# Fifteen one-word reads at the end of the first pass and seven one-word stores behind the last store of a channel-attention kernel

## The chip, the cores and the metric

The kernel runs on one core of a Trainium2 chip. The metric is the device time of one execution in microseconds (us). Runs of one kernel are told by their median, and one further execution is recorded by the hardware profiler, instruction by instruction. Times inside the profile count from the start of its span.

## What is computed

An image x of 384 x 384 pixels with 384 channels (bfloat16, 113 MB) is scaled channel by channel. The scale comes from the mean and the maximum of each channel over all pixels, through a small two-layer net:

```python
def reference(x, w1, w2):
    B, H, W, C = x.shape
    xf = x.reshape(B, H * W, C)
    gap = jnp.mean(xf, 1)
    gmp = jnp.amax(xf, 1)
    h_a = gap @ w1
    h_a = h_a * (lambda x, dt: x.astype(dt))(h_a > 0, h_a.dtype)
    h_m = gmp @ w1
    h_m = h_m * (lambda x, dt: x.astype(dt))(h_m > 0, h_m.dtype)
    scale = _sigmoid(h_a @ w2 + h_m @ w2)
    return x * scale[:, None, None, :]
```

No output can be written before the last pixel has been read. So x has to be read once for the scale, and whatever of it could not be kept in on-chip memory has to be read again.

## The kernel before

The 147,456 pixels lie as 1152 rows in each of 128 partitions (a "row" below is 384 channels, 768 bytes, in each partition). On-chip memory holds about 290 rows at a time, so the kernel makes two passes.

**First pass (loop at L363 to L396).** A list called steps is written out ahead of time: loads of blocks of rows into places of one large buffer (rows), and between them tests and packings. For each load the SP queue issues one transfer (L371). PE adds the rows up into a PSUM bank (L274) and DVE takes the running maximum into acc (L340), both as the load lands. One part of x (224 rows) is packed on the fly to seven blocks of 24 rows in place of 32 and stays on chip; its check and packing are ACT's and PE's work (L301, L302, L322, L328, L329). The order of every engine's instructions is that of the program text. There are 53 loads. Towards the end they get smaller, down to 2 to 11 rows, and they stay on chip for the second pass. The last four of them (SUM_TAIL) are summed by other matmuls (L290), and ahead of the last two (FOLD_BEFORE) DVE begins to fold acc (L355 to L357).

**The joint (L399 to L431).** The weights are loaded, acc is folded to one row, turned over by PE, reduced by DVE, and the small net gives z; ACT's sigmoid writes scale_bc (L431). Rows whose places were needed meanwhile (acc's own, and one block more) are read again (L412, L415).

**Second pass (L440 to L581).** DVE multiplies each block by scale_bc (L436), ACT's queue stores it (L445, L451, L490), and SP's queue reads the rows that were not kept (L529), each into a place whose store has landed. Packed blocks are unpacked between them by DVE (L468, L473) and ACT (L487). Three large stores of unpacked blocks go out among the last three blocks, and two small stores (L580, L581) come last. Behind these stands a branch (L582) that is entered only if the packing was not exact for some value; it reads a flag that the first pass computed.

**Queues and semaphores.** Loads are issued by SP, stores by ACT, each in program order. Every transfer, on either queue, signals its landing on one of eight semaphores (DMAHW0 to DMAHW7), which transfers take in turn in the order of the program. A transfer is issued when the one that had its semaphore before, eight places earlier, has landed, and when its other waits (a place to come free, say) are over:

```python
        _, block, rows, lo, hi = st
        m = hi - lo
        nc.sync.dma_start(out=rows, in_=rows_of(xr, block)[:, lo:hi, :])
...
    for to, block in leaving:
        store(to, block, 0)
    with tc.If(bad != 0):
```

Of the kernel before, what the change touches and what calls it, by code (L numbers as in the profile page):

```python
# [12 lines left out]
BF16 = mybir.dt.bfloat16  # L13
# [67 lines left out]
OTHER_PLACES = ((1, 17, (14,)), (2, 10, (24,)))  # L81
TEST_SCALE = 0.031187
SUM_TAIL = 4
MM_ROWS = 4


@with_exitstack
def kernel(
# [7 lines left out]
    nc = tc.nc  # L96
    P = nc.NUM_PARTITIONS
# [9 lines left out]
    xr = x.rearrange("b h w c -> (b h w) c")  # L107
    orr = out.rearrange("b h w c -> (b h w) c")

    def rows_of(ap, block):  # L110
        first, n = block
        return ap[first * P:(first + n) * P, :].rearrange("(p n) c -> p n c", n=n)

    consts = ctx.enter_context(tc.tile_pool(name="consts", bufs=1, side="right"))
# [5 lines left out]
    def take(n):  # L120
        nonlocal at
        at += n
        return at - n, n

    for_psum = PSUM_ROWS + BANK_ROWS
    first_block = take(for_psum + A)
# [14 lines left out]
    small = consts.tile([P, 16], BF16)  # L141
# [41 lines left out]
    late = words_ps[:, 0:LATE_ROWS, :]  # L183
    sum_ps = bank_a[0:NQP, 0:MM_ROWS * P]
    tp_ps = [
# [72 lines left out]
    loads = [st for st in steps if st[0] == "load"]  # L258
    tail_rows = sum(st[4] - st[3] for st in loads[len(loads) - SUM_TAIL:])

# [9 lines left out]
    def sums(rows, n, done, total):  # L270
        for k in range(0, n, MM_ROWS):
            g = min(MM_ROWS, n - k)
            for q in range(CQ):
                nc.tensor.matmul(  # L274
                    sum_ps[q * QP:q * QP + 1, 0:g * P],
                    lhsT=ones_bf[:, 0:1],
                    rhs=rows[:, k:k + g, q * P:(q + 1) * P],
                    start=(done + k == 0),
                    stop=(done + k + g == total),
                )  # L280

    def turn_sums():
        for r in range(MM_ROWS):
            nc.scalar.copy(out=s_sb[r % 2], in_=sum_ps[:, r * P:(r + 1) * P])  # L284
            nc.tensor.matmul(gsum_ps, lhsT=s_sb[r % 2], rhs=pick, start=(r == 0), stop=False)

    def tail_sums(rows, n, last):
        for k in range(n):
            for q in range(CQ):
                nc.tensor.matmul(  # L290
                    gsum_ps[:, q:q + 1], lhsT=rows[:, k, q * P:(q + 1) * P], rhs=ones_bf,
                    start=False, stop=(last and k == n - 1 and q == CQ - 1),
                )
# [12 lines left out]
    def test(i, what):  # L306

        if what == 2:
            test_one(high(part(i, 3), I8), 5 * i + 4)
            return  # L310
        n = G * C // 2
        a_b = homes[i][:, 0:2 * G, :].rearrange("p (r n) c -> p r (n c)", r=2).bitcast(I8)
        test_one(a_b[:, :, 2 * n * what + 1:2 * n * (what + 1):2], 5 * i + 2 * what)
        test_one(high(part(i, 2), I8)[:, n * what:n * (what + 1)], 5 * i + 2 * what + 1)

    def pack(i, half):
        n = G * C // 2
        span = slice(half * n, (half + 1) * n)
        for c in range(0, n, BANK):
            for r in range(4):  # L320
                for k, dt in enumerate((E4, E3)):
                    nc.tensor.matmul(  # L322
                        words[:, c:c + BANK], lhsT=weights[2 * r + k],
                        rhs=high(part(i, r), dt)[:, half * n + c:half * n + c + BANK],
                        start=(r == 0 and k == 0), stop=(r == 3 and k == 1),
                    )
        for r in (0, 1):
            nc.scalar.copy(out=high(part(i, r), U8)[:, span], in_=low(part(i, r + 2), U8)[:, span])  # L328
        nc.scalar.activation(  # L329
            out=part(i, 2).rearrange("p n c -> p (n c)").bitcast(U16)[:, span], in_=words,  # L330
            func=ACT.Copy, bias=32767.5,
        )

    def judge():
        nc.scalar.activation(out=test_copy, in_=tests[:, 0:NT], func=ACT.Copy, accum_out=test_sum)
        nc.scalar.copy(out=total, in_=test_sum)
        nc.tensor.matmul(bad_ps, lhsT=total, rhs=ones_bf, start=True, stop=True)

    def maximum(out_, in0, in1):
        nc.vector.tensor_tensor(out=out_, in0=in0, in1=in1, op=ALU.max)  # L340

    def turn_over(out_, rows):

        for r in range(LATE_ROWS):
            for q in range(CQ):
                nc.tensor.transpose(  # L346
                    out=out_[:, r, q * P:(q + 1) * P], in_=rows[:, r, q * P:(q + 1) * P], identity=ident_bf
                )
# [3 lines left out]
    def fold():  # L352

        n = folds[-1]
        h = n // 2  # L355
        maximum(acc[:, 0:h, :], acc[:, 0:h, :], acc[:, n - h:n, :])
        folds.append(n - h)  # L357

    done = turn = nth = 0
    for st in steps:  # L360
        if st[0] == "test":
            test(*st[1:])
        elif st[0] == "pack":  # L363
            pack(*st[1:])
        elif st[0] == "judge":
            judge()
        if st[0] != "load":
            continue
        _, block, rows, lo, hi = st
        m = hi - lo  # L370
        nc.sync.dma_start(out=rows, in_=rows_of(xr, block)[:, lo:hi, :])  # L371
        if nth < len(loads) - SUM_TAIL:
            sums(rows, m, done, TOT - tail_rows)
        else:
            tail_sums(rows, m, nth == len(loads) - 1)
        if nth == len(loads) - FOLD_BEFORE:
            fold()
        halves = HALVES if len(folds) == 1 else ((0, folds[-1]),)
        j = max(0, min(m, A - done))
        if j:  # L380
            nc.vector.tensor_copy(out=acc[:, done:done + j, :], in_=rows[:, 0:j, :])
        done += m
        if nth == len(loads) - SUM_TAIL - 1:
            turn_sums()
        while j < m:
            c, e = halves[turn % len(halves)]
            turn += 1
            e = min(e, c + m - j)
            maximum(acc[:, c:e, :], acc[:, c:e, :], rows[:, j:j + e - c, :])
            j += e - c  # L390
        if block == late_block:
            turn_over(late, rows)
        elif block == first_block:
            nc.vector.tensor_copy(out=kept_ps.bitcast(U32), in_=rows[:, 0:PSUM_ROWS, :].bitcast(U32))
            nc.vector.tensor_copy(out=kept_b.bitcast(U32), in_=rows[:, PSUM_ROWS:for_psum, :].bitcast(U32))
        nth += 1  # L396
# [37 lines left out]
    def multiply(dst, src):  # L434
        n = dst.shape[1]
        nc.vector.tensor_tensor(  # L436
            out=dst, in0=src, in1=scale_bc.unsqueeze(1).to_broadcast([P, n, C]), op=ALU.mult
        )
# [50 lines left out]
    def store(buf, block, lo):  # L489
        nc.scalar.dma_start(out=rows_of(orr, block)[:, lo:lo + buf.shape[1], :], in_=buf)  # L490
# [88 lines left out]
    assert not again and not order and not jobs  # L579
    for to, block in leaving:  # L580
        store(to, block, 0)  # L581
    with tc.If(bad != 0):  # L582
        for i in range(PACKED):
            for buf, lo in ((homes[i], FIRST_AT[i]), (homes_d[i], FOURTH_AT[i])):
                n = buf.shape[1]
                nc.sync.dma_start(out=buf, in_=rows_of(xr, packed_block)[:, lo:lo + n, :])
                multiply(buf, buf)
                store(buf, packed_block, lo)
# [30 lines left out]
```

## Time and profile before

| what | value |
|---|---|
| median of 3 runs | 725.78 us (725.48 to 726.16) |
| profiled execution, its own time | 725.41 us |
| span of the profile | 723.6 us |
| busy: DVE, ACT, PE | 564.1, 349.8, 184.7 us |
| read from DRAM, written to DRAM | 192.14 MB, 113.25 MB |
| mean rate over the span | 422 GB/s |
| granted clock of TensorE, mean | 0.616 |
| last load of the first pass issued | 255.65 us |
| scale_bc written | from 275.68 us, 0.49 us |
| last store issued | 681.52 us |

How to read what follows: in the strips the span, or a window of it, is cut into 40 equal slices, and a digit is the busy share in tenths (9 is 90% or more); DMA is the mean over the core's 16 DMA engines. The chain is the work that ended last, followed back from the end. In a list of waits, "A <- B: 36.6, 12, 11.6" says that A's engine stood 36.6 us in all for B, 12 times, at most 11.6 us. SPq and ACTq are the queues of SP and ACT that issue transfers. The trace also holds each update of a semaphore; a load or store makes 16 of them, one by one as its parts land.

### The profile page before, as it was taken

Reading aid. Unit: us, or ns where it says so; the run is one execution under the profiler, and the core shown is the slowest. Engines: PE = TensorE matmul, PEld = TensorE weight load, DVE = VectorE, ACT = ScalarE, POOL = GpSimd, SP = SyncE. Lnnn points to the kernel's source line nnn. Section 1 sums busy time; section 2 is a strip of 40 time slices with the busy share of each in tenths; the row PEclk is TensorE's granted clock in tenths of the full one; section 3 lists DMA queues with packets and bytes.
Section 4 is the critical chain, followed back from the end, with each engine's and each line's share of the span. In section 5 each row is a group of like instructions: output and inputs, shape, how many; then the busy total and the mean of one; then the engine's idle time right before and its main releaser. Section 6 shows DMA issues by size and latency. Waiting matters only on the chain.

```text
span 723.6 us, 3882 instructions
## 1 busy us (share of the span) xinstructions
PE 184.7 (26%) x1363; PEld 74.2 (10%) x1363; DVE 564.1 (78%) x445; ACT 349.8 (48%) x251; POOL 0.7 (0%) x6
## 2 busy tenths in 40 slices
PE   5577475965867470000000000000000000001000
PEld 1222122322322140000000000000000000001000
DVE  5699899999999998797966554897888889495200
ACT  6999999997999200056230023806154442200000
POOL 0000000000000000000000000000000000000000
PEclk9888878896988555555555555555555555555555
DMA  9999999999999979999999999999999999999997
GB/s 380 434 438 435 417 442 427 429 430 432 431 426 428 426 312 356 400 433 431 433 431 431 434 428 431 434 430 435 430 429 432 437 432 430 430 433 439 442 426 339
DMA packets 20403, 305.63 MB, mean 422 GB/s; under 512 B 2624, under 2 KB 2976, under 8 KB 7200
## 3 DMA queue, kind: packets, MB, share of 16 engines
q1 hardware_dynamic: 13040, 192.14, 62.3%
q10 hardware_dynamic: 7344, 113.25, 36.6%
q8 instruction: 10, 0.16, 0.1%
q14 instruction: 9, 0.07, 0.0%
HBM read 192.14 MB, written 113.25 MB: 422 GB/s over the span
## 4 chain that ended last, share of the span: by engine, by line
DMA 63%; DVE 25%; issue 3%; PE 2%; ACT 1%; SPq 0%; DVEq 0%; ACTq 0%
DMA rows<-in_x_dram 40%; DMA out_dram<-rows 23%; DVE acc L340 16%; DVE rows L436 9%; PE words_ps L322 1%; ACT rows L328 0%; DVE acc L436 0%; SPq L371 0%; PE bank_a L274 0%; ACT rows L329 0%; ACT rows L487 0%; PE bank_a L430 0%; ACT scale_bc L431 0%; DVE small L424 0%; PE bank_a L423 0%
## 5 line engine op out<-in xcount | busy, mean ns | idle before, releaser
L436 DVE TENSOR_TENSOR rows<-rows,scale_bc 128x9216 bf16<-128x9216 bf16 (+9 forms) x56 | 230.9, 4164 | 91.2 <-DMA rows<-in_x_dram 90.0
L340 DVE TENSOR_TENSOR acc<-acc,rows 128x2304 bf16<-128x2304 bf16 (+4 forms) x227 | 245.0, 1154 | 13.9 <-DMA rows<-in_x_dram 13.6
L487 ACT COPY rows<-rows 128x1536 uint8<-128x1536 uint8 x28 | 41.3, 1476 | 204.2 <-DVE rows L436 144.8
L274 PE MATMUL bank_a<-rows,small 128*1 128x512 bf16 (+3 forms) x897 | 93.3, 466 | 80.9 <-DMA rows<-in_x_dram 76.1
L346 PE MATMUL words_ps<-ident_bf,acc 128*128 128x128 bf16 x24 | 2.7, 310 | 376.3 <-DVE acc L574 376.3
L301 ACT ACTIVATE rows<-rows 128x3072 uint8<-128x3072 int8 (+1 forms) x35 | 81.9, 2341 | 9.1 <-DMA rows<-in_x_dram 8.4
L302 ACT ACTIVATE rows<-rows 128x3072 uint8<-128x3072 uint8 (+1 forms) x35 | 82.0, 2344 | 1.1
L487 ACT COPY rows<-acc 128x1536 uint8<-128x1536 uint8 x42 | 60.5, 1473 | 18.2 <-DVE acc L473 17.7
L274 PEld LDWEIGHTS <-small 128*1 128x1 bf16 x897 | 30.6, 95 | 140.3 <-issue 118.2
L346 PEld LDWEIGHTS <-acc 128*128 128x128 bf16 x24 | 2.5, 144 | 376.7 <-DVE acc L574 376.7
L322 PE MATMUL words_ps<-rows,scale_bc 128*128 128x512 fp8e4 (+1 forms) x126 | 37.9, 414 | 9.2 <-ACT rows L329 9.2
L328 ACT COPY rows<-rows 128x1536 uint8<-128x1536 uint8 x28 | 39.7, 1468 | 0.4 <-PE words_ps L322 0.4
L322 PE MATMUL words_ps<-rows 128*128 128x512 fp8e3 (+1 forms) x126 | 35.8, 394 | 0.0
L468 DVE TENSOR_SCALAR rows<-rows 128x1536 uint16<-128x1536 uint16 x56 | 31.3, 560 | 1.9
L322 PE MATMUL words_ps<-rows,w_sb 128*128 128x512 fp8e3 x84 | 27.0, 405 | 0.0
L487 ACT COPY acc<-rows 128x1536 uint8<-128x1536 uint8 x14 | 20.5, 1466 | 0.0
L329 ACT ACTIVATE rows<-words_ps 128x1536 uint16<-128x1536 f32 x14 | 20.1, 1439 | 0.0
L322 PEld LDWEIGHTS <-scale_bc 128*128 128x128 bf16 x126 | 12.2, 103 | 30.2 <-issue 19.3
L322 PEld LDWEIGHTS <-rows 128*128 128x128 bf16 x126 | 12.9, 102 | 16.7 <-issue 3.3
L473 DVE SCALAR_TENSOR_TENSOR acc<-acc,rows 128x768 uint32<-128x768 uint32 x14 | 13.4, 959 | 0.5
L473 DVE SCALAR_TENSOR_TENSOR rows<-rows 128x768 uint32<-128x768 uint32 x14 | 13.4, 958 | 0.5
L284 ACT COPY w_sb<-bank_a 65x128 f32<-65x128 f32 x2 | 0.5, 261 | 24.5 <-PE bank_a L274 24.0
(61 smaller groups left out, 72.0 us busy)
## 6 DMA issues: line engine op xcount, KB each, us to landing
rows<-in_x_dram SPq DMA_DIRECT2D x16, 2880.0 KB, 25.4
out_dram<-rows ACTq DMA_DIRECT2D x15, 2880.0 KB, 22.8
rows<-in_x_dram SPq DMA_DIRECT2D x15, 2304.0 KB, 20.0
out_dram<-rows ACTq DMA_DIRECT2D x14, 2304.0 KB, 21.1
rows<-in_x_dram SPq DMA_DIRECT2D x4, 3072.0 KB, 31.8
out_dram<-rows ACTq DMA_DIRECT2D x2, 4608.0 KB, 46.7
rows<-in_x_dram SPq DMA_DIRECT2D x9, 768.0 KB, 16.7
rows<-in_x_dram SPq DMA_DIRECT2D x2, 3264.0 KB, 26.4
```

The lines of the kernel that those rows point to most:

```text
L274: nc.tensor.matmul(sum_ps[q * QP:q * QP + 1, 0:g * P], lhsT=ones_bf[:, 0:1], rhs=rows[:, k:k + g, q * P:(q + 1) * P], start=(done + k == 0 ...
L301: nc.scalar.activation(out=out_, in_=rows, func=ACT.Square, bias=test_bias, scale=TEST_SCALE)
L302: nc.scalar.activation(out=out_, in_=out_, func=ACT.Square, bias=minus4, accum_out=tests[:, k:k + 1],)
L322: nc.tensor.matmul(words[:, c:c + BANK], lhsT=weights[2 * r + k], rhs=high(part(i, r), dt)[:, half * n + c:half * n + c + BANK], start=(r ...
L328: nc.scalar.copy(out=high(part(i, r), U8)[:, span], in_=low(part(i, r + 2), U8)[:, span])
L329: nc.scalar.activation(out=part(i, 2).rearrange("p n c -> p (n c)").bitcast(U16)[:, span], in_=words, func=ACT.Copy, bias=32767.5,)
L340: nc.vector.tensor_tensor(out=out_, in0=in0, in1=in1, op=ALU.max)
L346: nc.tensor.transpose(out=out_[:, r, q * P:(q + 1) * P], in_=rows[:, r, q * P:(q + 1) * P], identity=ident_bf)
L436: nc.vector.tensor_tensor(out=dst, in0=src, in1=scale_bc.unsqueeze(1).to_broadcast([P, n, C]), op=ALU.mult)
L468: nc.vector.tensor_scalar(out=u16(dst), in0=u16(src), scalar1=s1, scalar2=s2, op0=op0, op1=op1)
L473: nc.vector.scalar_tensor_tensor(out=u32(v), in0=u32(v), scalar=0x3F3F3F3F, in1=u32(m), op0=ALU.bitwise_xor, op1=ALU.bitwise_xor)
L487: nc.scalar.copy(out=dst, in_=src)
```

## The change

Two lists are added, a small tile and a small tensor in DRAM. Behind five of the last 20 loads of the first pass (the 20th, 18th, 17th, 14th and 12th from the end), SP issues three reads each. A read takes one word (two bfloat16 channels) of x into each of k partitions, every eighth one from the first on; k goes over 1 to 15. The words land in probe_sb, a column of its own for each read, and nothing uses them. Behind the last store, ACT issues seven stores of one word from each of k = 2, 4, ... 14 partitions of the tile small into the scratch tensor probe_dram. The computation and the output stay the same.

```diff
+PROBES = {20: (1, 2, 3), 18: (5, 6, 7), 17: (9, 10, 11), 14: (13, 14, 15), 12: (4, 8, 12)}
+PROBES_AT_END = (2, 4, 6, 8, 10, 12, 14)
...
+    probe_sb = consts.tile([P, 40], BF16)
+    probe_dram = nc.dram_tensor("probe", [P, 40], BF16).ap()
+    probed = 0
+
+    def probe(k):
+        nonlocal probed
+        c = 2 * probed
+        probed += 1
+        nc.sync.dma_start(
+            out=probe_sb[0:8 * k:8, c:c + 2], in_=rows_of(xr, first_block)[0:8 * k:8, 0, 2 * probed:2 * probed + 2]
+        )
+
     done = turn = nth = 0
...
         nc.sync.dma_start(out=rows, in_=rows_of(xr, block)[:, lo:hi, :])
+        for k in PROBES.get(len(loads) - nth, ()):
+            probe(k)
         if nth < len(loads) - SUM_TAIL:
...
     for to, block in leaving:
         store(to, block, 0)
+    for i, k in enumerate(PROBES_AT_END):
+        c = 2 * i
+        nc.scalar.dma_start(out=probe_dram[0:8 * k:8, c:c + 2], in_=small[0:8 * k:8, 2:4])
     with tc.If(bad != 0):
```

Each of the 22 added transfers takes a semaphore of the eight in its turn.

## The prediction

> **What bounds the kernel now.** I read the strips of the page first, then the split of the chain, then windows of both ends of the change. The profiled execution took 725.41 us (its span 723.6 us, 1.8 us around it); the median of the three runs is 725.78, so this execution stands 0.37 us below it.
>
> ```profile
> DVE  5699899999999998797966554897888889495200
> DMA  9999999999999979999999999999999999999997
> GB/s 380 434 438 435 417 442 427 429 430 432 431 426 428 426 312 356 400 433 431 433 431 431 434 428 431 434 430 435 430 429 432 437 432 430 430 433 439 442 426 339
> ...
> DMA 63%; DVE 25%; issue 3%; PE 2%; ACT 1%; SPq 0%; DVEq 0%; ACTq 0%
> ```
>
> The DMA engines are busy in every slice (18 us each) and move about 430 GB/s, except in the two or three slices from 253 us on: the joint between the passes. So the time is transfers, end to end, plus that joint. The reads of the change lie just before the joint, the stores behind the last transfer. Both places need a look of their own. First the windows (busy us, with counts, of each engine, then PE clock, DMA share, GB/s):
>
> ```profile
> core 0: us, PE busy (x) PEld busy (x) DVE busy (x) ACT busy (x) POOL busy (x), PEclk, DMA share, GB/s
> ...
> 240.00:264.00 24.00, 13.55 (x97) 3.81 (x96) 23.13 (x23) 0.19 (x1) 0.00 (x0) 0.50 1.01 424
> 264.00:277.00 13.00, 8.05 (x111) 7.15 (x105) 10.75 (x17) 1.78 (x7) 0.00 (x0) 0.50 0.65 222
> ```
>
> In the last 24 us of the first pass DMA is full, but DVE has 23.13 busy us too. The chain through the joint tells which is later:
>
> ```profile
> 267.02 1.03 DVE acc L340 x2
> 268.05 0.02 issue
> 268.07 1.17 DVE acc L340
> 269.24 0.02 issue
> 269.26 1.37 DVE acc L340
> 270.63 0.04 DVEq L340
> ```
>
> It is DVE after DVE. Beside it I set each load's last semaphore update. The load issued at 242.80 landed at 258.15, and DVE was free for it at 258.55; the next at 260.46 against 260.89; the last two at 267.16 and 268.33 against 269.2 and 270.6. So a load may land **0.40 us** later here at no cost, the last two over 2 us.
>
> Third, the drain of the load queue, 264 to 280 us in slices of 0.4 us:
>
> ```profile
> DMA  9987643172106000974979999995599600397997
> ```
>
> It does not stop at once: 16 semaphore updates belong to each load, and from 230 us on the last comes 3.1 to 3.2 us after the first (2.0 us before 229 us). One of 16 engines is late, and the landing counts the latest.
>
> **The reads.** PE, DVE and POOL keep their instructions in their order. SP gains 15 issues at L371's place, behind the loads issued now at 202.04 (reads of 1, 2, 3 partitions), 216.40 (5, 6, 7), 221.73 (9, 10, 11), 230.38 (13, 14, 15) and 232.77 us (4, 8, 12). Nothing reads what they bring. They cost in three ways.
>
> *On the rings.* The trace has no 4-byte data packet. Its 4-byte semaphore packets take 9 ns, the smallest data packets (192 bytes, first weights) 15 ns at the median and 234 ns at most. I take one of 15 and one of 9, 24 ns a read, for it is a packet of that kind in a queue that runs on: at most 15 x 24 = 0.36 us if the late engine gets all 15, nothing if it gets none. That is under the cover of 0.40 us, so **0**; by 9 + 9 it is 0.27, by 234 + 9 it is 3.6, less the cover 3.2 us. The cover is DVE's work; without it the 0.36 would stand in full. Below zero I see nothing: no byte is taken away.
>
> The Trainium skill (DMA: Bandwidth & Descriptors, "Why a DMA increments its semaphore by 16 and not by 1") says that a transfer goes over the largest number of engines up to 16 that divides its slowest dimension, on SP's queue the lowest-numbered ones. By that the first engine gets all 15 reads and the sixteenth none, and the term is 0 to 0.36 by the late engine's number, which no view tells; the sum stays.
>
> *On SP.* Issues take 0.33 us behind a wait, 0.42 to 0.46 one after another, and 1.64 once (second weights). I take 0.45, nearest to loads in a row: 1.4 us for three reads, 4.9 at the upper end.
>
> *On the eight semaphores.* Transfers take eight semaphores in turn, and each waits until the one eight places before has landed. This is the wait to look at:
>
> ```profile
> SPq L371 <- DVE acc L340: 36.6, 12, 11.6
> SPq L371 <- DMA rows<-in_x_dram: 8.1, 4, 2.2
> ```
>
> (window 200 to 270 us: total, times, longest). For instance the issue at 251.04 follows the landing at 251.02 of the load issued at 234.74. A read takes a place like a load of 1.5 MB, so fewer bytes are in flight. Going down the new order with the old landings: the read of 7 waits for 220.45, which delays nobody (the load behind it goes at 221.73, for DVE). The load now issued at 222.16 waits for the landing at 227.48 of the load of 216.40: **5.3 us later**. At 227.5 the queue holds one load alone, the one of 221.73, done between 228.65 on the first engine and 230.67 on the last. A new issue reaches its first packet after 1.0 us (269.74 to 270.72, 0.74 to 1.77), so at 228.5: just in time for the first engine, 2 us early for the last. Then the read of 12 waits for 241.47, and the loads of 234.74, 237.74 and 239.02 go at about 242.0, 242.4 and 242.9, **7.2 us later** at worst. The queue then holds the loads of 231.24 and 232.77, which end at 245.36 on the first engine and 248.51 on the last: 2.4 us to spare. The next ones go at 245.15, 248.55, 249.0, 249.4 and 249.9, and from 251.04 on the old times return. DVE and PE behind them wait for landings, and these do not move while the queue isn't empty. SP's issues, even at 1.64 us, fall into these waits (at 241.5, for one: 243.1 plus 1.0 is still before 245.36). Cost **0**; what hides it is the data queued ahead, and without it each us of idle queue over the 2 us of the late engine costs one.
>
> **The second pass** starts from scale_bc at 276.20 as before; its waits for semaphores are the same ones, one semaphore earlier in the turn. Cost 0.
>
> **The stores.** They are queued on ACT behind the last store (issued 681.52, landed 721.61) and wait for the landings of the transfers eight before: 677.50, 684.30, 695.21, 702.02, 712.90, 717.46, and for the seventh 719.77. So six go unseen and the seventh is issued at 719.8, 1.8 us before the end. On an empty ACT queue the first store went from issue at 277.00 to its first packet at 277.88 and to landing 0.35 us after its last packet:
>
> ```profile
> out_dram<-rows ACTq DMA_DIRECT2D x1, 288.0 KB, 2.1
> ...
> scale_bc<-in_w_dram SPq DMA_DIRECT2D x1, 72.0 KB, 3.2
> ```
>
> (KB, us from issue to landing). A word would so land at 719.8 + 0.88 + 0.02 + 0.35 = 721.05, under the last store; behind the late engine's last packet it comes 0.03 later. SP then takes the semaphores one by one, 0.09 each, perhaps one more behind the last store. I take **+0.2 us**; the lower end is +0.0, the upper the row of 3.23 us: 723.03, +1.4. Nothing else waits for ACT there.
>
> **Sum:** 725.41 + 0 + 0 + 0 + 0.2 = 725.6 for an execution like the profiled one, and 0.37 more at the median: **726.0 us**. A measurement of this kernel tells about 0.2% (1.45 us) from no change.
>
> **The rivals.**
> 1. *Each small read holds its ring, and the first pass ends later (slower).* Place: the late engine's ring between 202 and 250 us. At the longest 192-byte packet, 234 + 9 ns, 15 reads make 3.6 us, less 0.4 of cover: 726.0 + 3.2 = 729.2. It decides from (1.45 + 0.4)/15 = 0.12 us a read. Against it: the load of 192 KB issued at 251.04 landed 0.49 us behind its predecessor, and its bytes alone take 0.46 at 430 GB/s; a transfer as such holds nothing. For it: there is no row of a word. Chance 0.10.
>    [...]
> 2. *The last word lands late.* With 3.23 us from issue, 727.2 to 727.4. For it: a word into DRAM is no row here; against it: 2.1 us for a whole store. Chance 0.12, half of it within 0.2%.
> 3. *The eight semaphores empty the queue.* If the issue at 227.5 takes 3.2 us to reach the rings (as to landing above), the late engine idles for 0.03 us, the first one for 2; even 1 us more gives only 727.0. Chance 0.04, a quarter of it slower.
> 4. *Less lag among the engines (faster).* Another rhythm of issues could leave the late engine less late: at the joint DVE stands in the way, at the end the 16 updates are 1.33 us apart, so at most 1.3 us: 724.7. Chance 0.04, half of it beyond 0.2% with luck in the second pass.
>
> **Numbers.** The forecast has 0.70, all within 0.2%. Same: 0.70 + 0.06 + 0.03 + 0.02 = 0.81; slower: 0.10 + 0.06 + 0.01 = 0.17; faster 0.02. The range runs from 725.2 (runs spread 0.35 to either side, and a part of rival 4) to 727.5 (rival 2); the rest of rival 1 and of rival 4 stays outside.
>
> **What would show it.** Reads: 15 issues of SP in 202 to 242 us, the load of 222.16 at about 227.5, that of 234.74 at about 242; GB/s of 200 to 264 us unchanged near 425; the sigmoid's scale_bc within 0.4 us of 276.2. A gap in the DMA strip near 228 would speak for rival 3, a later scale_bc with a full strip for rival 1. End: the seventh store issued near the third-last landing, and the last landing 1.9 to 2.1 us before the span's end, as now. Wrong it would be above all if a word on a ring costs far more than a packet of 192 bytes.

## The result and the profile after

The changed kernel takes **727.41 us** (median of 9 runs, 726.64 to 728.25), the kernel before 725.69 (9 runs on the same chip): +1.72 us, a ratio of 1.0024 with a 95% interval of 1.0014 to 1.0034. The forecast was 726.0 us; the time lies inside its range, 0.09 us under the upper end. The profiled execution of the changed kernel took 728.25 us, the longest of its nine, so what is read from it is some 0.8 us more than the median. Lines have moved: the load is L386, a read of the change L370, the maximum L343, the multiplication L453, a store of the change L601, the branch L602.

The strips of the page, and the split of its chain:

```profile
span 726.4 us, 3902 instructions
...
DVE  6699899999999998797966453898888889495200
...
DMA  9999999999999978999999999999999999999997
GB/s 383 432 443 424 429 428 432 432 430 431 431 425 416 424 300 351 390 435 429 431 436 426 434 427 434 427 430 434 434 430 434 433 430 433 433 433 442 431 430 321
...
DMA 64%; DVE 25%; issue 2%; PE 1%; ACT 1%; SPq 0%; DVEq 0%; ACTq 0%
```

At this scale nothing has happened: two slices below 9 at the joint, and the last one with 321 GB/s in place of 339. So both ends of the change have to be opened. First SP, window 200 to 250 us of the changed kernel (start, duration of the row, what is issued; a row that holds several issues also holds the waits between them):

```profile
216.71 4.23 SPq L370 DMA_DIRECT2D probe_sb<-in_x_dram  x3
221.69 0.34 SPq L386 DMA_DIRECT2D rows<-in_x_dram  x1
222.07 2.33 SPq L370 DMA_DIRECT2D probe_sb<-in_x_dram  x3
227.37 2.26 SPq L386 DMA_DIRECT2D rows<-in_x_dram  x3
...
237.12 6.44 SPq L370 DMA_DIRECT2D probe_sb<-in_x_dram  x3
243.67 6.60 SPq L386 DMA_DIRECT2D rows<-in_x_dram  x5
```

The load that went at 222.16 goes at 227.37, the next group at 243.67 in place of 234.74. SP's waits (window 200 to 270 us; total, times, longest) say for whom:

```profile
SPq L386 <- DVE acc L343: 17.5, 3, 10.7
SPq L386 <- DMA rows<-in_x_dram: 12.7, 7, 3.0
SPq L370 <- DMA rows<-in_x_dram: 10.3, 4, 3.9
```

Of 36.6 us behind DVE 17.5 are left; the waits for a landing, whose semaphore the next transfer needs, grew from 8.1 us to 23.0. What the load at 227.37 found is in the windows (columns as in the prediction; the first row is the kernel before, the other three the changed kernel):

```profile
220.00:240.00 20.00, 13.56 (x96) 5.11 (x96) 19.71 (x20) 19.82 (x15) 0.00 (x0) 0.76 1.01 430
...
220.00:240.00 20.00, 13.43 (x96) 5.01 (x96) 17.80 (x18) 19.81 (x16) 0.00 (x0) 0.80 1.01 417
240.00:264.00 24.00, 12.33 (x88) 3.58 (x90) 23.73 (x23) 0.16 (x1) 0.00 (x0) 0.50 1.01 423
264.00:277.00 13.00, 9.25 (x117) 7.36 (x111) 11.30 (x16) 1.29 (x6) 0.00 (x0) 0.50 0.62 211
```

13 GB/s less over 20 us are 0.26 MB, 0.6 us at full rate. The busy share does not show it (1.01 both times), the bytes do. DVE, which works on what has landed, has 1.91 us less to do in these 20 us (17.80 against 19.71). In the next 24 us it makes up 0.60 of them (23.73 against 23.13), and the other 1.31 are what the joint is late. The chain of the changed kernel there:

```profile
268.36 1.03 DVE acc L343 x2
269.38 0.02 issue
269.41 1.17 DVE acc L343
270.58 0.02 issue
270.60 1.37 DVE acc L343
271.97 0.04 DVEq L343
```

Piece for piece it is the chain of before, 1.34 us later. The drain of the load queue, 264 to 280 us in slices of 0.4 us:

```profile
DMA  9999973002063100500092899999968689740089
```

It is full up to 266.0 us where it had been falling from 264.8 on: most engines now end closer together, and later. The last update of the last load still comes 3.4 us behind its first (3.1 before).

The span grew from 723.63 to 726.43 us. Its parts, from the semaphore updates in the trace of both:

| place | before | after | growth |
|---|---|---|---|
| first store of the second pass issued (the joint) | 277.00 | 278.34 | 1.34 |
| last store of the output landed | 721.61 | 723.74 | 2.13, so 0.79 in the second pass |
| last word landed | - | 724.68 | 0.94 |
| from the last landing to the span's end | 2.02 | 1.75 | -0.27 |

Four terms, in one execution. Which of them are the change's, and which are chance, could only be told by other kernels.

### The profile page after: what moved, and what is told of

It reads as the page before. It is cut to its first block, busy times and chain, and to the rows that moved or that the text cites. A ratio compares the mean times of both kernels' runs of the same rounds, so it can differ in the third digit from the quotient of the medians.

```text
span 726.4 us, 3902 instructions
## 1 busy us (share of the span) xinstructions
PE 185.4 (26%) x1363; PEld 74.2 (10%) x1363; DVE 564.2 (78%) x445; ACT 349.8 (48%) x251; POOL 0.7 (0%) x6
## 4 chain that ended last, share of the span: by engine, by line
DMA 64%; DVE 25%; issue 2%; PE 1%; ACT 1%; SPq 0%; DVEq 0%; ACTq 0%
DMA rows<-in_x_dram 40%; DMA out_dram<-rows 24%; DVE acc L343 16%; DVE rows L453 9%; PE words_ps L325 1%; ACT rows L331 0%; DVE acc L453 0%; SPq L386 0%; PE bank_a L277 0%; ACT rows L332 0%; PE bank_a L447 0%; ACT scale_bc L448 0%; DVE small L441 0%; PE bank_a L440 0%; PE bank_a L445 0%
## 5 line engine op out<-in xcount | busy, mean ns | idle before, releaser
L453 DVE TENSOR_TENSOR rows<-rows,scale_bc 128x9216 bf16<-128x9216 bf16 (+9 forms) x56 | 230.9, 4164 | 93.5 <-DMA rows<-in_x_dram 91.7
L343 DVE TENSOR_TENSOR acc<-acc,rows 128x2304 bf16<-128x2304 bf16 (+4 forms) x227 | 245.0, 1156 | 15.4 <-DMA rows<-in_x_dram 15.1
```

The lines of the kernel that those rows point to most:

```text
L453: nc.vector.tensor_tensor(out=dst, in0=src, in1=scale_bc.unsqueeze(1).to_broadcast([P, n, C]), op=ALU.mult)
```

## The experiments

Each kernel is timed against the kernel before on the same chip; given are the medians of all runs, and a ratio with its 95% interval. The ratio is not always the quotient of the two medians (1.0019 for the seven stores alone, where the ratio is 1.0014). "Joint" is the issue of the second pass's first store (277.00 us before).

### The two halves

The reads alone (the loop of the seven stores taken out):

```diff
-    for i, k in enumerate(PROBES_AT_END):
-        c = 2 * i
-        nc.scalar.dma_start(out=probe_dram[0:8 * k:8, c:c + 2], in_=small[0:8 * k:8, 2:4])
```

> The fifteen reads alone, without the seven stores. In the profile of the changed kernel the sigmoid comes 1.3 us later and the last landing of the seven stores 0.94 us behind that of the last real store. If the reads cost at the joint (theory A: the load held to 227.4 us reaches an almost empty queue; theory B: every word holds its ring by some 0.09 us) this one is about 0.8 to 1.3 us above the kernel before, 726.5 to 727.0, with the sigmoid at about 277.0 in place of 275.7. If the stores cost it all, it is at 725.7.

The stores alone:

```diff
-PROBES = {20: (1, 2, 3), 18: (5, 6, 7), 17: (9, 10, 11), 14: (13, 14, 15), 12: (4, 8, 12)}
+PROBES = {}
```

> The seven stores alone, without the reads. Theory C: the words land one behind another, 0.19 us apart, behind the last real store, so the end comes 0.7 to 1.0 us later: 726.4 to 726.7, the joint as before. By the prediction's own step they cost 0.0 to 0.2: 725.7 to 725.9. Rival: no cost of their own, what was seen at the end belongs to a disturbed second pass: 725.7.

Reads alone: 725.75 us against 725.61, ratio 1.0001 (0.9991 to 1.0011). Stores alone: 726.96, ratio 1.0014 (1.0004 to 1.0023), +1.35 us. So at the median the larger part is the stores, the term that the forecast put at 0.2.

The reads' profile shows the same late load, issued at 227.25, and the same lost bytes:

```profile
220.00:240.00 20.00, 13.42 (x96) 4.99 (x96) 18.89 (x19) 19.79 (x16) 0.00 (x0) 0.83 1.01 418
240.00:264.00 24.00, 12.74 (x97) 3.64 (x96) 23.87 (x24) 0.00 (x0) 0.00 (x0) 0.55 1.01 424
264.00:277.00 13.00, 7.91 (x111) 6.99 (x105) 10.76 (x17) 1.78 (x7) 0.00 (x0) 0.63 0.66 233
```

418 GB/s as in the changed kernel, and yet the joint is at 276.98: it was the early engines that lost, and the late one, which the landings count, did not. Its lag behind the first, 3.1 us before, is 2.2 to 2.6 us here (3.4 to 3.7 in the changed kernel). DVE has all but 0.08 us of its work done by 264 us (18.89 + 23.87 against 19.71 + 23.13). The twelve runs of this kernel fall in two groups, seven from 725.45 to 725.80 and five from 726.34 to 726.66. A loss that comes in some executions would look like this, but the groups do not show one: the runs of the kernel with three words behind the last store, which holds no load, also fall into 725.49 to 725.77 and 726.11 to 726.56.

In the stores' profile the last store of the output lands at 722.19, and the seven words are as follows (us; a landing is the last of a transfer's updates):

| word in k partitions | 2 | 4 | 6 | 8 | 10 | 12 | 14 |
|---|---|---|---|---|---|---|---|
| issued | 684.49 | 685.68 | 695.76 | 702.57 | 713.47 | 718.02 | 720.32 |
| landed | 721.97 | 722.37 | 722.55 | 722.73 | 722.91 | 723.09 | 723.26 |

From k = 4 on they come 0.18 us apart, whether a word was issued 37 us earlier or 3. The strip of this kernel from 720 to 726 us, in slices of 0.15 us:

```profile
DMA  9899976310000000000000000000000200000000
GB/s 532 369 410 451 451 328 206 83 41 0 41 1 1 0 0 0 0 0 0 0 0 0 0 0 0 0 0 0 0 0 0 55 0 0 0 0 0 0 0 0
```

The last packet is over before 721.95 (the 55 at 724.65 is a fetch of instructions). The 1.3 us behind it hold no bytes, only updates of semaphores; the last updates of the words come one each 0.18 us.

### The reads: which of them, and what an empty queue costs

Without the reads of 9, 10 and 11 partitions, which make the load of 222.16 wait, and without the stores:

```diff
-PROBES = {20: (1, 2, 3), 18: (5, 6, 7), 17: (9, 10, 11), 14: (13, 14, 15), 12: (4, 8, 12)}
+PROBES = {20: (1, 2, 3), 18: (5, 6, 7), 14: (13, 14, 15), 12: (4, 8, 12)}
```

> Twelve reads: those by 9, 10 and 11 partitions are left out, and the stores too. Without them the load that was held to 227.4 us goes at about 222 again, but the later hold (to about 242) stays, with two loads ahead in the queue. Theory A: the joint is back within 0.3 us of before, 725.7 to 726.1. Theory B: twelve fifteenths of the loss stay, about 726.4 to 726.8.

725.17 us, ratio 0.9988 (0.9979 to 0.9998). The load goes at 222.02 as before, the joint is at 277.00. The loads behind it are still held, to 242.34, but with two loads queued ahead of them. Twelve reads cost nothing; the kernel is even faster, for which see the end of the program below.

The same load held without any read or store: a copy of one word on POOL makes it wait for the landing of the load of 216.40, the event that held it in the changed kernel.

```diff
+HOLD = {16: 2}
...
+        if len(loads) - nth in HOLD:
+            seen = loads[nth - HOLD[len(loads) - nth]][2]
+            nc.gpsimd.tensor_copy(out=rows[0:1, 0, 0:2], in_=seen[0:1, 0, 0:2])
         nc.sync.dma_start(out=rows, in_=rows_of(xr, block)[:, lo:hi, :])
```

> No reads and no stores of a word. A copy of one word by GpSimd from the place of the load issued at 216.4 to the place of the load issued at 222.16 (which overwrites it) makes that load wait for the landing at 227.4, as the reads do. Theory A: 1.0 to 1.4 us later at the joint, 726.6 to 727.1. Theory B: nothing is on the rings, so 725.7.

The load goes at 228.81 (the copy adds 1.3 us to the landing at 227.49), the joint is 0.51 us later, the time 726.16 against 725.61, ratio 1.0001 (0.9990 to 1.0013). That is between the 725.7 and the 726.6 to 727.1 expected by the two theories. The runs do not tell it from no change; the trace does show the late joint.

Held until the queue is surely empty, behind the load of 221.73:

```diff
-HOLD = {16: 2}
+HOLD = {16: 1}
```

> As the run with one load held, but the copy reads the place of the load issued at 221.7, so the load behind it goes only when that one has landed, at about 230.6, and the queue runs dry for certain. Theory A (what costs is a load that reaches an empty queue): 1.0 us to the first packet and 0.5 to 1 us until it streams, from 230.3 on the late engine, less 0.4 us of cover, so 1.2 to 2.0 us above the kernel before, in nearly every run: 726.8 to 727.6. If late issues do not matter at all: 725.6.

728.98 us, ratio 1.0047 (1.0033 to 1.0061). The strip from 224 to 240 us, in slices of 0.4 us:

```profile
DMA  9969899999865500001000969499999898999999
GB/s 465 507 292 499 357 426 430 430 430 430 349 269 242 215 0 0 0 0 41 0 0 0 261 163 261 163 392 424 490 424 424 359 412 340 376 405 430 445 488 434
```

The last engine is done at 230.28, the load goes at 232.03, the first bytes move in the slice from 232.8 us (the 41 ahead of it is a fetch of instructions), and four slices pass before 390 GB/s are reached. The joint is at 280.02, 3.0 us later, more than the 1.2 to 2.0 us expected. So a load that finds the queue empty costs time at the joint. One profile each gives 0.5 us for the issue at 228.8 and 3.0 at 232.0; at 227.3 three profiles give 0 to 1.34.

Four reads, the first of the fifteen, no stores:

```diff
+PROBES = {20: (1, 2, 3), 18: (5,)}
```

> Four reads (1, 2, 3 and 5 partitions) and no stores: no load is held, but the last real store has the last of the eight semaphores, as in the run without the reads by 9 to 11. Theory D (SP takes the eight semaphores one by one in a fixed order, and those behind the last landing cost 0.07 to 0.09 us each): 0.3 to 0.45 us below the kernel before, 725.1 to 725.3. Rival (twelve reads helped through another rhythm of the loads): 725.6.

725.62 us, ratio 0.9997 (0.9983 to 1.0011), joint at 276.76. The same number of reads far from the joint, behind the 43rd load from the end:

```diff
+PROBES = {43: (1, 2, 3, 5)}
```

> Four reads (1, 2, 3 and 5 partitions) behind the eleventh load, and nothing else. Nothing near the joint changes, but the last real store has the last of the eight semaphores and SP's program is longer. Theory D (the end of SP's program: four fewer semaphores behind the last landing, and no pause of 0.4 us before the last ones): 725.0 to 725.3, below the kernel before. Rival (reads near the joint did it): 725.6.

725.37 us, ratio 0.9995 (0.9986 to 1.0004), joint at 277.00. In these two kernels no load is held, in that with twelve reads only those with data queued ahead of them, and neither place nor number of the reads costs anything.

### The stores: late issue, late landing, or a price of each word

One store (the word in 14 partitions), no reads:

```diff
+PROBES_AT_END = (14,)
```

> No reads and one store of a word (14 partitions) in place of seven. It is issued at about 685 us, long before the end. Theory C (each small store takes 0.18 us on the rings behind the last real store): +0.2 to +0.4, 725.8 to 726.0. Rival (what costs is that the last word is issued 1.8 us before the end): 725.6. Rival (a small store behind the last one costs about 1 us as such): 726.7.

725.58 us, ratio 0.9999 (0.9990 to 1.0008). Issued at 684.60, landed 0.20 us behind the last store of the output.

Seven words again, each from all 128 partitions, no reads:

```diff
-        nc.scalar.dma_start(out=probe_dram[0:8 * k:8, c:c + 2], in_=small[0:8 * k:8, 2:4])
+        nc.scalar.dma_start(out=probe_dram[:, c:c + 2], in_=small[:, 2:4])
```

> No reads; the seven stores write one word from all 128 partitions, in place of every eighth one up to 14. Theory C by engines (0.18 us a store on each engine that takes part, whatever its bytes): as with the seven small ones, 726.7 to 727.1. Theory C by packets (the time goes with the packets, now eight on each engine): up to eight times, 0.18 x 8 x 7 = 10 us, 735. Theory of odd counts (only transfers on fewer than 16 engines are slow): 725.7.

728.37 us, ratio 1.0037 (1.0024 to 1.0051), +2.6 us, where 726.7 to 727.1 was expected. The words land at 723.12, 723.31, 723.49, 723.67, 723.85, 724.03 and 724.21: 0.18 apart again, now all seven behind the last store of the output (722.93). 9 times as many partitions (128 against 14) do not change the 0.18. What I had not expected is that the last store itself is late: its 16 updates spread over 2.11 us, those of the stores ahead over 0.95 to 0.98. This accounts for the other 1.3 us; its cause stays open.

Three words behind the last store, and the same three ahead of it (no reads in both):

```diff
-PROBES_AT_END = (2, 4, 6, 8, 10, 12, 14)
+PROBES_AT_END = (10, 12, 14)
```

For the second kernel also:

```diff
-    for to, block in leaving:
-        store(to, block, 0)
+    store(leaving[0][0], leaving[0][1], 0)
     for i, k in enumerate(PROBES_AT_END):
...
+    store(leaving[1][0], leaving[1][1], 0)
```

> No reads; three stores of a word (10, 12 and 14 partitions) behind the last real store. Theory C, now as a floor (the last update of a transfer comes 0.18 us or more after that of the transfer ahead of it on the same engines, which shows only where no bytes cover it): last landing 0.55 us behind that of the last real store, 726.0 to 726.2. Rival (the cost lies in being issued late: the third one goes at about 702 us, early enough): 725.6.

> The same three stores ahead of the last real store, whose 768 KB take 1.8 us. Floor theory: covered, 725.5 to 725.8. Rival (each small store takes 0.18 us of its rings, wherever it stands): as three behind, 726.0 to 726.2. The last real store is issued at about 695 us in place of 682, with 24 us of stores ahead of it in the queue, which should cost nothing.

Behind: 725.77 us, ratio 1.0006 (0.9997 to 1.0015); the words land at 721.71, 721.89 and 722.07 behind the store's 721.53. Ahead: 725.51, ratio 0.9995 (0.9986 to 1.0004); the words land at 720.67, 720.86 and 721.05 behind the 720.49 of the store before them, and the last store at 722.31, 1.82 behind that one, where it was 1.83 behind with no word between. So a word adds nothing to the landings while bytes run beside it, and 0.18 us when nothing does. At the level of whole runs three words behind the last store are not told from none.

### The changed kernel once more

> The changed kernel once more, for a second profile. If the joint's 1.3 us came by chance (a late load sometimes finds the late engine idle, sometimes not), the sigmoid stands anywhere from 275.6 to 277.1 and the runs spread over 726.6 to 728.3; the words at the end land 0.18 us apart again. If the joint is always late, it is at 277.0 again.

727.72 us, ratio 1.0029 (1.0018 to 1.0039). In this profile (727.19 us) the load goes at 227.33, the joint is 0.46 us late, and the words end 0.93 us behind the last store.

```profile
220.00:240.00 20.00, 13.32 (x96) 5.00 (x96) 18.40 (x18) 19.80 (x16) 0.00 (x0) 0.76 1.01 416
240.00:264.00 24.00, 13.06 (x94) 3.77 (x96) 23.90 (x24) 0.00 (x0) 0.00 (x0) 0.50 1.01 424
```

The lost bytes are the same again, but DVE is only 0.54 us of work behind at 264 us (18.40 + 23.90 against 42.84). The end of the words repeats to 0.01 us, the joint does not.

## Why the forecast held, and where it failed

**Reads on the rings: right.** The forecast had 24 ns a read and 0 after the cover, the first rival 0.12 us a read and more. Three reads (5, 6 and 7 partitions) lie between two loads in the changed kernel; the second load still lands 3.20 us behind the first (3.19 before). The next pair with reads between them (13, 14 and 15) lands 3.65 apart (3.63 before). The page cited for the number of engines (the Trainium skill, DMA: Bandwidth & Descriptors, "Why a DMA increments its semaphore by 16 and not by 1") left open whether the late engine gets all the reads or none. The trace settles it: the read by 13 partitions lands at 240.33 with the early engines, that by 14 at 242.97 with the late one, and likewise in the other profiles with these reads. So the engine that is late from 234 us on has two of the fifteen. That agrees with the rule that a transfer by k partitions takes the k lowest-numbered engines; the numbers themselves are not in the trace. Rival 1 falls.

**Reads on SP: too cheap, without effect.** An issue of a read takes 0.33 to 0.82 us (median 0.72), not 0.45. The 0.3 us more went into waits, as the forecast had it.

**The eight semaphores: right mechanism, right times, and a size that only chance made right.** The load of 222.16 was forecast for 227.5 and went at 227.37; the loads of 234.74 and after for about 242 and went at 243.67 (242.32 where the joint was not late). The cost was put at 0, and three profiles of this hold show 0, 0.46 and 1.34 us at the joint. The forecast's own sign for the joint, scale_bc within 0.4 us of 276.2, is missed in the changed kernel, where it is written by 277.52. The step that failed is "so at 228.5: just in time for the first engine, 2 us early for the last". The first packet did go at 228.43, 1.06 us after the issue. But eight of the first nine packets took 0.70 to 1.13 us, in place of the 0.49 of packets of their size in a queue that runs on. So the engines that were done early lost time although they count as busy (the 0.6 us of lost bytes above). Nor does the last engine, at 230.48, tell which one the joint will wait for: ten of the 16 finish between 229.63 and 230.48. Of the held load's 16 updates, 15 are in by 234.39 us (234.76 in the second profile, 234.22 with reads alone); the last comes at 237.10 (236.38, 235.89), and the joint is late by 1.34 (0.46, 0). So one engine decides, and the 2 us counted to the last one at 230 us were no reserve to count on. Why it is later in one run than in another stays open. Rival 3 had the right mechanism at the right place, and 727.0 as its most; at the median the reads alone are worth 0.14 us (725.75 against 725.61).

**The stores: the term that was mis-sized.** +0.2 was forecast; the stores alone measure +1.35 at the median (about 1.0 by the ratio, 0.3 to 1.7). The forecast's picture of issues was right (the seventh goes at 720.32 in the kernel with stores alone, 0.02 us behind the landing it waits for). It failed at "behind the late engine's last packet it comes 0.03 later" and at "six go unseen". What a word adds is not its packet but a place in a row of landings 0.18 us apart. Five or six words come behind the last store of the output: 5 x 0.19 = 0.94 in the changed kernel, 6 x 0.18 = 1.08 in that with stores alone. What the stores' median has beyond this is not accounted for. The theory that the seventh issue is late falls with the issue times above; that of a long way from issue to landing (the second rival's 3.23 us) falls with the first words, issued some 37 us before they land and just as late. Rival 2 gave the right time, 727.2 to 727.4, for the wrong reason. That the measured time lies in the range is luck to that extent: the range reaches to 727.5 for rival 2 alone, and the sum itself stood at 726.0.

The same page (the Trainium skill, DMA: Bandwidth & Descriptors), in "Anatomy of one DMA", has most of a transfer's fixed 2.0 us in the receipt of its last byte, longest when the target is DRAM. That section is about transfers issued by GpSimd, and those of this kernel are issued by SP and ACT. The page's table "Latency and other measured facts" gives 0.2 us on average for an access to DRAM, and 2 us at high load. The 0.18 us are of the size of a receipt at 0.2 us for each word; that the words wait for receipts is not shown by any run here, and the reads of the change, which land in on-chip memory, keep the same distance (227.42, 227.60, 227.79), which speaks against DRAM as its cause. At that section's 2.0 us each, one after another, seven words would have made 14 by estimate; no run shows that.

**The end of the program: not in the forecast.** Behind the last landing SP takes eight semaphores in a fixed order, then the final ones, mostly 0.06 to 0.10 us each. Two things differ among the kernels. One is the place of the last semaphore in this order: six are left behind the last word of the changed kernel, four behind the last store before, none in the kernels with 12 or 4 reads. The other is a pause of 0.40 us, which stands in eight of the fourteen profiles, those without reads. In the same eight, and in no other, a packet of the queue of instructions moves some 0.6 us after the pause begins; for the kernel before (window 715 to 730 us):

```profile
q14 instruction: 1, 0.01, 0.1%
```

The way from the last landing to the end is so 2.02 us before, 1.68 with reads alone, and 1.31 to 1.32 with 12 or 4 reads. For this reason too one word costs less than its 0.20 us: behind the last store's landing the program ends 2.15 us later with it and 2.02 without. The times show less than the 0.7 us: with four reads the medians are 0.16 and 0.27 us below the kernel before, no difference by their intervals, where 0.3 us and more was expected; in both profiles the second pass is as much longer. And so the reads give back what they cost, in part: with twelve of them the kernel is 0.12% faster (0.02 to 0.21%), the only version here whose interval lies below the kernel before.

**The sum.** Reads alone and stores alone make +1.5 us, both together +1.72 and, the second time, +2.08. The 0.2 to 0.6 us between are within what the joint's chance can do, and not settled. The 0.79 us that the second pass took longer in the changed kernel's profile can't be laid to the change: from the joint to the last landing of the output it is 0.62 to 0.78 us longer in the four profiles with reads alone, 0.60 with the seven stores alone, 0.73 with three words ahead of the last store, and 0.80 in the kernel with one load held, which adds no transfer. It is 0.06 longer with one word and 0.27 with three behind. What sets this was not found. The forecast gave 0.81 to a time within 0.2% of the kernel before and 0.17 to a slower one; the measured ratio, 1.0024, is just beyond 0.2%, and its interval reaches below; with the stores at their measured price the forecast's own sum is 726.0 - 0.2 + 1.35 = 727.15 us.

## What to carry to other kernels

Put small stores ahead of the last large one: three there cost nothing here, and seven behind it cost 0.93 to 1.08 us of landings, one behind another, when no bytes were left to move. When each transfer takes one of a few semaphores in turn, a word takes the place of a megabyte: go down the new order and ask which large load it holds, and what is queued when that load is issued. A reserve counted to the last engine is no reserve for the others, so look at bytes moved and not at the busy share, and at more than one profile.

## What the runs showed of the hardware that was not expected

- Words that follow one another on one queue land one after another, in these profiles mostly 0.18 us apart and never less than 0.15, for loads and stores, for 2 partitions and 128.
- A load that meets an empty or nearly empty queue starts slowly: its first packet comes 0.95 to 1.06 us after the issue, and early packets then take up to 1.70 us in place of 0.49 (the load issued at 227.25 with reads alone).
- How far the late engine lies behind the others is carried along a full queue to the end of the pass: 3.1 us before, 2.2 to 2.6 with reads alone, 1.5 and 1.0 where the load was held longer. Before, the lag grows from 2.0 to 3.2 us when a packet of 16 KB of the instruction queue runs (0.96 us, from 234.38); where that packet fell into the emptied queue (231.44) the lag is 1.0.
- In the profiles with reads the end of the program lacks a pause of 0.40 us; that the longer program of SP is the reason is argued, not shown. The place of the last transfer's semaphore among the eight moves the end by up to 0.45 us (six of them behind the last word of the changed kernel, 724.69 to 725.14).
